# A fused attention and expert kernel: last batch's tiles reordered, an input split spread out, first step given more projection work

## The chip, the cores and the metric

One core of one Trainium2 chip runs the whole program. The metric is device time in microseconds for one execution, as the median of several runs.

## The reference

Three layers follow each other on four sequences of 576 tokens. The first two (windowed attention with 8 heads, then a gated layer with a spatial mix) are not touched by the change. The third is the one at issue:

```python
logits = x @ w_gate                      # 4 experts, the best 2 are kept, softmax over them
for e in range(E):
    q, k, v = x @ wq[e], x @ wk[e], x @ wv[e]
    a = softmax(causal(scale * (q @ k.T)))
    out += gate[e] * (a @ v @ wo[e])     # gate is 0 for experts that were not kept
```

Each expert is thus one causal attention head of width 64 over 576 tokens, weighted by a gate for each token.

## The kernel before, in words

The first 336 us compute the first two layers and the fold of their last weight into the projections. The change touches only what follows, the third layer, called stage B here.

Stage B has 20 tiles: four batches of five tiles of query rows, tiles 0 to 3 with 128 rows each and tile 4 with the last 64 rows (two experts stand side by side in it). Tile j sees j + 1 blocks of 128 keys, so tile 0 is the smallest and tiles 3 and 4 the largest. Tile 4 of two neighbouring batches share one output tile, so an even batch's tile 4 has no output work of its own.

The loop over s (L957) runs 22 steps. Step s does, in this order: `attend_b` of tile s - 2 (the product with v, into pxB, L906), the first half of `scores_b` of tile s (psB, L845, for tile 4 L847), `take_b` of tile s - 2 (pxB split into a rounded high part by ACT, L132, and a remainder by DVE, L129), and then five rounds, in each of which it takes some dense work (`dense.pull`), one group of up to four transposes of tile s - 1 (`turn_b`: TensorE into ptB, L888, copied to pTB by ACT or DVE, L889), and in two of the rounds the softmax of a half of tile s (`softmax_b`). The softmax of a half is a DVE operation with a running minimum (L150, for tile 4 L859), an exponential with row sums on ACT (L151, L861), then for both halves together L866 to L868 on DVE (sum, reciprocal, times the gate of the token), and the scaling of each row block by POOL (`scale_rows`, L158). The transposes read what POOL has scaled.

The dense work is a queue of generators: the projections of the next batch (`proj`: q and k, 12 matmuls of 288 columns for each half row, L780, evicted by ACT L784 and DVE L129; v and gate logits, L804, evicted by ACT L808) and the output tiles (`out_tile`: six matmuls of 512 columns, L927, evicted by ACT L941, written by SP L943). A unit is four of these matmuls (two in an output tile). `dense.pull(RATE / 5)` adds to a credit and hands out units until it is used up, so RATE is the dense work of a step in ns by the kernel's own count (488 for a unit of q or k). RATE is 3700 to step 14 and 4400 from there.

At the end of a projection `gates` computes the token gates of its batch from the logits (DVE L746 to L759, with one small POOL operation, L154, and a reciprocal, L155). Step 0 differs from the other steps that begin a batch: batch 0 was projected just ahead of the loop, so its gates are computed while step 0 runs, and L868 of tile (0, 0) waits for them.

`load_g` reads the input of a batch two ahead from memory (L699, L700) and splits it into a rounded part and a remainder, in four pieces: ACT L704 and DVE L129 for each, named x<-gf. They are handed out by `next(gparts)` in the rounds. The split of batch 3 overwrites what the projection of batch 1 reads, so it can't run before that has ended.

TensorE's instructions stand in the order in which the program calls them. For ACT, DVE, POOL and SP a scheduler sets the order when the kernel is built. The PSUM pools hold one score tile (psB), two tiles for transposes (ptB), one for pxB and three for dense work.

```python
for i in range(5):
    dense.pull((RATE if s < 15 else 4400.0) / 5)
    next(turn, None)
    ...
    if s < 15:
        next(gparts, None)
```

Of the kernel before, what the change touches and what calls it, by code (L numbers as in the profile page):

```python
# [21 lines left out]
B, H, S, D = 4, 8, 576, 64  # L22
# [80 lines left out]
def block_kernel(ctx, tc, qP, kP, v, w_in, wspT, bsp, w_outT, wcat, wo, rel, relt, low, tri, out):  # L103
    nc = tc.nc
# [20 lines left out]
    dense = Dense()  # L125
# [401 lines left out]
    tiles = [(b, j) for b in range(B) for j in range(5)]  # L527
# [75 lines left out]
    RATE = 8200.0  # L603
    outw = iter(())
    for s in range(2, len(tiles) + 2):
# [6 lines left out]
        if s > 2:  # L612
            b, j = tiles[s - 2]
# [306 lines left out]
    def out_tile(b, t):  # L920
        t0, tn = TOK[t][0], P
        o2 = OT.pop((b, t))
        po = psD.tile([P, 512], F32, tag="D", name=f"pout{b}_{t}")
        n = 0
        for i, j in PASSES:
            for pr in range(2):
                nc.tensor.matmul(po[:tn], o2[i][:, pr, :tn], wos[j][:, pr, :], start=(n == 0), stop=(n == 5))  # L927
                n += 1
            if n < 6:
                yield 2 * 216  # L930
        ot = wk.tile([P, DM], F32, tag="ot", name=f"ot{b}_{t}", bufs=3)
        if (b, t) == (B - 1, 4):

            for h, copy in enumerate((nc.scalar.copy, nc.vector.tensor_copy)):
                c = slice(256 * h, 256 * h + 256)
                copy(ot[:, c], po[:, c])  # L936
                for i in range(2):
                    (nc.sync, nc.scalar)[i].dma_start(out[b - 1 + i, t0:S, c], ot[64 * i : 64 * i + 64, c])
            yield 2 * 216
            return  # L940
        nc.scalar.copy(ot[:tn], po[:tn])  # L941
        if t < 4:
            nc.sync.dma_start(out[b, t0 : t0 + tn, :], ot)  # L943
        else:
            for i in range(2):
                nc.sync.dma_start(out[b - 1 + i, t0:S, :], ot[64 * i : 64 * i + 64])
        yield 2 * 216

    tiles = [(b, j) for b in range(B) for j in range(5)]
    dense.add(proj(0, G), 18000.0)  # L950
    G, gparts = load_g(1, gfp)
    for _ in gparts:
# [2 lines left out]
    RATE = 3700.0  # L955
    px = None
    for s in range(len(tiles) + 2):  # L957
        if s < len(tiles):
            b, j = tiles[s]
            if j == 0:  # L960
                dense.through(f"p{b}")
                for _ in gparts:
                    pass
                if b + 1 < B:
                    dense.add_front(proj(b + 1, G), 18000.0, f"p{b + 1}")
                if b + 2 < B:
                    G, gparts = load_g(b + 2, gfp)
        if s >= 2:
            px = attend_b(*tiles[s - 2])
        if s < len(tiles):  # L970
            scores_b(*tiles[s], 0)
        if s >= 2:
            b1, j1 = tiles[s - 2]
            take_b(b1, j1, px)
            if j1 < 4 or b1 % 2:
                dense.add(out_tile(b1, j1), 1300.0)
        turn = turn_b(*tiles[s - 1]) if 1 <= s <= len(tiles) else iter(())
        for i in range(5):
            dense.pull((RATE if s < 15 else 4400.0) / 5)
            next(turn, None)  # L980
            if s < len(tiles) and i == 0:
                softmax_b(*tiles[s], 0)
            if s < len(tiles) and i == 2:
                scores_b(*tiles[s], 1)
                softmax_b(*tiles[s], 1)
            if s < 15:
                next(gparts, None)
    dense.drain()

# [71 lines left out]
```

## Time and profile before

| | us |
|---|---|
| median of 3 runs (lowest to highest) | 515.16 (515.05 to 515.49) |
| the profiled execution, whole | 514.89 |
| its span, first to last recorded instruction | 513.2 |
| TensorE's matmuls busy in the span | 488.0 |

The page gives the busy time of each engine over the span. In a timeline each row is a run of equal instructions of one engine: start in us, length in us until the last of them has ended, engine, line, operation, tiles, shape and count, and in square brackets how long the engine had been idle and what released it. Matmuls are pipelined: the next row of TensorE starts some 0.1 to 0.25 us before the row ahead has ended, so the cost of a row is the distance from its start to the next row's start.

### The profile page before, as it was taken

How to read it: one execution, taken by the hardware profiler on the slowest of the kernel's cores; microseconds unless marked ns; L12 is line 12 of the kernel's file. 1: busy time of each engine (PE TensorE's matmuls, PEld its weight loads, DVE VectorE, ACT ScalarE, POOL GpSimd, SP SyncE). 2: the span in 40 equal slices, each digit the busy share in tenths (PEclk: the TensorE clock that was granted, in tenths of full speed). 3: DMA queues.
4: the chain of work that ended last, by engine and by line, in shares of the span. 5: the costliest groups of instructions: out<-in, count | busy, mean ns of one | idle time of the engine just before them, and what ended most of it. 6: DMA issues, size and time to landing. Idle time of an engine off the chain costs nothing. (4 is left out here: it accounts for less than half of the span.)

```text
span 513.2 us, 10541 instructions
## 1 busy us (share of the span) xinstructions
PE 488.0 (95%) x3910; PEld 425.5 (83%) x3910; DVE 308.4 (60%) x1069; ACT 261.8 (51%) x778; POOL 98.4 (19%) x205
## 2 busy tenths in 40 slices
PE   8879889999999999999999999989989999999995
PEld 6547668898988989899888999978978898897784
DVE  4978877555878768785455525264574564562441
ACT  4764567533656337463344314264564554546652
POOL 0012210222102211012211010122322333232121
PEclk9997989999999999999999999999999999999999
DMA  8931223325231451301206640230000000003321
GB/s 283 372 128 42 63 87 102 114 70 181 91 94 43 180 189 42 94 2 52 104 1 193 198 158 5 90 93 1 1 1 3 2 1 1 1 2 116 112 103 42
DMA packets 25079, 44.34 MB, mean 86 GB/s; under 512 B 5826, under 2 KB 8258, under 8 KB 24644
## 3 DMA queue, kind: packets, MB, share of 16 engines
q1 hardware_dynamic: 24868, 43.54, 25.4%
q8 instruction: 31, 0.51, 0.4%
q10 hardware_dynamic: 160, 0.13, 0.1%
q14 instruction: 20, 0.16, 0.1%
HBM read 32.13 MB, written 11.53 MB: 85 GB/s over the span
## 5 line engine op out<-in xcount | busy, mean ns | idle before, releaser
L151 ACT ACTIVATE p<-p,st 128x128 f32<-128x128 f32 x144 | 56.3, 392 | 38.0 <-DVE st L150 38.0
L436 PE MATMUL pv<-win,x 128*128 128x512 f32 x240 | 63.9, 409 | 0.7 <-ACT x L132 0.7
L780 PE MATMUL pq<-x,W 128*128 128x288 f32 x384 | 59.4, 303 | 0.9 <-DVE k L129 0.8
L516 PE MATMUL pg<-wsp,vn 128*128 128x288 f32 x384 | 58.9, 298 | 0.1
L780 PEld LDWEIGHTS pq<-x,W 128*128 128x128 f32 x384 | 52.1, 188 | 4.8 <-issue 2.3
L499 PE MATMUL pu<-x,win 128*128 128x288 f32 x384 | 55.1, 298 | 0.0
L398 POOL TENSOR_SCALAR_AFFINE_SELECT pU<-pT 128x512 f32<-128x512 f32 (+1 forms) x32 | 22.6, 706 | 168.1 <-ACT pT L391 164.1
L158 POOL TENSOR_SCALAR pB<-pB,stB 128x128 f32<-128x128 f32 (+4 forms) x72 | 39.0, 560 | 80.1 <-DVE stB L868 65.5
L516 PEld LDWEIGHTS pg<-wsp,vn 128*128 128x128 f32 x384 | 52.9, 188 | 1.3 <-issue 1.0
L499 PEld LDWEIGHTS pu<-x,win 128*128 128x128 f32 x384 | 52.0, 188 | 1.8 <-issue 0.5
L436 PEld LDWEIGHTS pv<-win,x 128*128 128x128 f32 x240 | 43.9, 192 | 9.8 <-issue 1.0
L151 ACT ACTIVATE pB<-pB,stB 128x128 f32<-128x128 f32 (+3 forms) x64 | 35.6, 558 | 13.6 <-DVE stB L150 13.6
L150 DVE CUSTOM_DVE_ANT_0 pB<-psB,trit 128x128 f32<-128x128 f32 (+3 forms) x64 | 28.3, 485 | 11.1 <-PE psB L845 10.5
L888 PE MATMUL ptB<-ident,pB 128*128 128x128 f32 (+1 forms) x200 | 31.1, 274 | 3.9 <-POOL pB L158 3.6
L804 PE MATMUL pvB<-W,x 128*128 128x260 f32 (+1 forms) x240 | 34.7, 289 | 0.0
L804 PEld LDWEIGHTS pvB<-W,x 128*128 128x128 f32 (+1 forms) x240 | 30.1, 178 | 1.1 <-issue 1.1
L927 PE MATMUL pout<-wo,o 128*128 128x512 f32 x108 | 30.1, 410 | 1.0 <-ACT o L132 1.0
L353 PE MATMUL ps<-k,q 64*128 64x256 f32 (+1 forms) x256 | 29.8, 374 | 0.8 <-DMA k<-in_kP 0.8
L390 PE MATMUL pt<-ident,p 128*128 128x128 f32 x144 | 22.9, 277 | 7.8 <-DVE x L129 6.1
L888 PEld LDWEIGHTS ptB<-ident,pB 128*128 128x128 f32 (+1 forms) x200 | 23.7, 139 | 7.6 <-POOL pB L158 4.7
L150 DVE CUSTOM_DVE_ANT_0 p<-ps,relm 128x128 f32<-128x128 f32 x128 | 29.5, 286 | 0.7 <-DMA relm<-in_rel 0.2
L415 PE MATMUL px<-pT,v 128*64 128x128 f32 (+1 forms) x320 | 29.6, 276 | 0.0
(147 smaller groups left out, 882.0 us busy)
## 6 DMA issues: line engine op xcount, KB each, us to landing
q<-in_qP SPq DMA_DIRECT2D x20, 256.0 KB, 3.0
g_dram<-g SPq DMA_DIRECT2D x16, 288.0 KB, 2.1
raw<-in_w_in SPq DMA_DIRECT2D x8, 512.0 KB, 6.8
v<-in_v SPq DMA_DIRECT2D x16, 256.0 KB, 3.2
gf<-g_dram SPq DMA_DIRECT2D x4, 1024.0 KB, 5.3
out<-ot SPq DMA_DIRECT2D x16, 256.0 KB, 2.0
k<-in_kP SPq DMA_DIRECT2D x3, 1152.0 KB, 5.3
rawo<-in_w_outT SPq DMA_DIRECT2D x4, 512.0 KB, 4.3
```

Of the source, the lines that this page charges most:

```text
L150: nc.vector.tensor_tensor_reduce(s_view, ps_view, tab, -0.125, FLT_MAX, ALU.add, ALU.min, nm)
L151: nc.scalar.activation(s_view, s_view, AF.Exp, bias=nm, scale=-1.0, accum_out=sm)
L158: nc.gpsimd.tensor_scalar(p, p, r, 0.0, op0=ALU.mult, op1=ALU.add)
L353: nc.tensor.matmul(ps[:, o, 256 * h : 256 * h + kn], Q_[b, j][r, hp, :], K_[b][r, hp, k0 : k0 + kn], start=True, stop=True)
L415: nc.tensor.matmul(px[64 * o : 64 * o + 64, hp, :qn], V_[b, t][:kb, h * 64 : h * 64 + 64], rhs, start=(t == max(0, j - 1)), stop=(t == j))
L436: nc.tensor.matmul(pv, x[i][:, k, t0 : t0 + P], win[j][:, k, 512:1024], start=(n == 0), stop=(n == 11))
L499: nc.tensor.matmul(pu[:, :HALF], win[i][:, k, m * P : (m + 1) * P], x[j][:, k, c], start=(n == 0), stop=(n == 11))
L516: nc.tensor.matmul(pg[:, :HALF], vn[i][k][:, m * P : (m + 1) * P], wsp[j][:, k, c], start=(n == 0), stop=False)
L780: nc.tensor.matmul(pq[:, :HALF], W[i][:, k, c0 : c0 + P], G[j][:, k, c], start=(n == 0), stop=(n == 11))
L804: nc.tensor.matmul(pv[:tn, :260], G[i][:, k, COL[t] : COL[t] + tn], W[j][:, k, 512:772], start=(n == 0), stop=(n == 11))
L888: nc.tensor.transpose(pt[:kb, n, :], p[pr][:, o, c0 : c0 + kb], ident)
L927: nc.tensor.matmul(po[:tn], o2[i][:, pr, :tn], wos[j][:, pr, :], start=(n == 0), stop=(n == 5))
```

## The change

Four edits, all in stage B. The tiles of the last batch (3) are taken in the order 3, 4, 2, 1, 0. The split of the input is handed out in rounds 1 and 3 of the steps that don't begin a batch, eight pieces over four steps, where it was one in every round from the beginning. In step 0 the dense credit is 5500 where it was 3700. And the last output tile, now tile 0 of batch 3 with 128 rows of one batch, is written as two halves of 256 columns, the first by SP and the second by ACT's queue, one transfer each, where the old last tile sent two transfers from each queue.

```diff
--- before.py
+++ after.py
@@ -929,13 +929,12 @@
             if n < 6:
                 yield 2 * 216
         ot = wk.tile([P, DM], F32, tag="ot", name=f"ot{b}_{t}", bufs=3)
-        if (b, t) == (B - 1, 4):
+        if (b, t) == tiles[-1]:
 
             for h, copy in enumerate((nc.scalar.copy, nc.vector.tensor_copy)):
                 c = slice(256 * h, 256 * h + 256)
                 copy(ot[:, c], po[:, c])
-                for i in range(2):
-                    (nc.sync, nc.scalar)[i].dma_start(out[b - 1 + i, t0:S, c], ot[64 * i : 64 * i + 64, c])
+                (nc.sync, nc.scalar)[h].dma_start(out[b, t0 : t0 + tn, c], ot[:, c])
             yield 2 * 216
             return
         nc.scalar.copy(ot[:tn], po[:tn])
@@ -946,7 +945,8 @@
                 nc.sync.dma_start(out[b - 1 + i, t0:S, :], ot[64 * i : 64 * i + 64])
         yield 2 * 216
 
-    tiles = [(b, j) for b in range(B) for j in range(5)]
+
+    tiles = [(b, j) for b in range(B) for j in ((3, 4, 2, 1, 0) if b == B - 1 else range(5))]
     dense.add(proj(0, G), 18000.0)
     G, gparts = load_g(1, gfp)
     for _ in gparts:
@@ -957,7 +957,7 @@
     for s in range(len(tiles) + 2):
         if s < len(tiles):
             b, j = tiles[s]
-            if j == 0:
+            if s % 5 == 0:
                 dense.through(f"p{b}")
                 for _ in gparts:
                     pass
@@ -976,14 +976,16 @@
                 dense.add(out_tile(b1, j1), 1300.0)
         turn = turn_b(*tiles[s - 1]) if 1 <= s <= len(tiles) else iter(())
         for i in range(5):
-            dense.pull((RATE if s < 15 else 4400.0) / 5)
+
+            dense.pull((5500.0 if s < 1 else RATE if s < 15 else 4400.0) / 5)
             next(turn, None)
             if s < len(tiles) and i == 0:
                 softmax_b(*tiles[s], 0)
             if s < len(tiles) and i == 2:
                 scores_b(*tiles[s], 1)
                 softmax_b(*tiles[s], 1)
-            if s < 15:
+
+            if s < 15 and s % 5 and i in (1, 3):
                 next(gparts, None)
     dense.drain()
```

**TensorE at the first two steps.** The piece from the last projection units of step 0 to the transposes of tile (0, 0). pq is a projection tile of batch 1, psB0_1 the scores of tile (0, 1), ptB0_0 the transposes of tile (0, 0). Before:

```order
L780 MATMUL pq1_0_0_0_3923<-x20_3582,W0_3250 128x288 x4
L780 MATMUL pq1_0_0_0_3923<-x21_3583,W0_3250 128x288 x4
L845 MATMUL psB0_1_0_3937<-k0_0_3612,q0_0_3614 128x256 x2
L845 MATMUL psB0_1_0_3937<-k0_1_3613,q0_0_3614 128x256 x2
L845 MATMUL psB0_1_0_3937<-k0_0_3612,q0_1_3615 128x256 x2
L845 MATMUL psB0_1_0_3937<-k0_0_3612,q0_0_3614 128x256 x2
L845 MATMUL psB0_1_0_3937<-k0_1_3613,q0_0_3614 128x256 x2
L845 MATMUL psB0_1_0_3937<-k0_0_3612,q0_1_3615 128x256 x2
L780 MATMUL pq1_0_0_0_3923<-x20_3582,W1_3251 128x288 x4
L780 MATMUL pq1_0_0_1_3960<-x20_3582,W0_3250 128x288 x4
L888 MATMUL ptB0_0_0_3965<-ident_72,pB0_0_0_3851 128x128 x2
L888 MATMUL ptB0_0_0_3965<-ident_72,pB0_0_1_3852 128x128 x2
```

After the change:

```order
L780 MATMUL pq1_0_0_1_3939<-x20_3582,W0_3250 128x288 x4
L780 MATMUL pq1_0_0_1_3939<-x21_3583,W0_3250 128x288 x4
L780 MATMUL pq1_0_0_1_3939<-x20_3582,W1_3251 128x288 x4
L845 MATMUL psB0_1_0_3956<-k0_0_3612,q0_0_3614 128x256 x2
L845 MATMUL psB0_1_0_3956<-k0_1_3613,q0_0_3614 128x256 x2
L845 MATMUL psB0_1_0_3956<-k0_0_3612,q0_1_3615 128x256 x2
L845 MATMUL psB0_1_0_3956<-k0_0_3612,q0_0_3614 128x256 x2
L845 MATMUL psB0_1_0_3956<-k0_1_3613,q0_0_3614 128x256 x2
L845 MATMUL psB0_1_0_3956<-k0_0_3612,q0_1_3615 128x256 x2
L780 MATMUL pq1_1_1_0_3970<-x20_3582,W0_3250 128x288 x4
L888 MATMUL ptB0_0_0_3975<-ident_72,pB0_0_0_3851 128x128 x2
L888 MATMUL ptB0_0_0_3975<-ident_72,pB0_0_1_3852 128x128 x2
```

Four more units stand ahead of the scores of (0, 1) and one fewer between them and the transposes: three more, all told, ahead of the transposes.

**DVE at the end of batch 0.** The rows from the split of batch 3 on. x21<-gf3 are its four remainders, pTB0_3 copies of transposes of tile (0, 3), stB0_4 the statistics of tile (0, 4), c1, c2 and mx the gates of batch 1. Before:

```order
L889 COPY pTB0_3_4_4277<-ptB0_3_4_4276 128x512
L859 ISA pB0_4_1_4238,stB0_4_4239<-psB0_4_1_4300,tritail_3255 128x288
L859 ISA stB0_4_4239 128x1
L859 ISA pB0_4_1_4238,stB0_4_4239<-psB0_4_1_4300,tritail_3255 128x288
L859 ISA stB0_4_4239 128x1
L889 COPY pTB0_3_12_4321<-ptB0_3_12_4320 128x512
L860 TENSOR_TENSOR stB0_4_4239<-stB0_4_4239 128x1
L129 TENSOR_TENSOR x21_3583<-gf3_4361,x20_3582 128x576 x4
L746 TENSOR_TENSOR c1_1_4332<-vt1_4142 128x80
L747 TENSOR_TENSOR c2_1_4333<-vt1_4142 128x80
L751 TENSOR_REDUCE mx1_4336<-vt1_4142 128x5
L866 TENSOR_SCALAR stB0_4_4239<-stB0_4_4239 128x2
```

After the change:

```order
L129 TENSOR_TENSOR x21_3583<-gf3_4373,x20_3582 128x576
L889 COPY pTB0_3_4_4294<-ptB0_3_4_4293 128x512
L129 TENSOR_TENSOR x21_3583<-gf3_4373,x20_3582 128x576 x2
L859 ISA pB0_4_1_4255,stB0_4_4256<-psB0_4_1_4339,tritail_3255 128x288
L859 ISA stB0_4_4256 128x1
L859 ISA pB0_4_1_4255,stB0_4_4256<-psB0_4_1_4339,tritail_3255 128x288
L859 ISA stB0_4_4256 128x1
L129 TENSOR_TENSOR x21_3583<-gf3_4373,x20_3582 128x576
L746 TENSOR_TENSOR c1_1_4301<-vt1_4114 128x80
L747 TENSOR_TENSOR c2_1_4302<-vt1_4114 128x80
L751 TENSOR_REDUCE mx1_4305<-vt1_4114 128x5
L889 COPY pTB0_3_12_4361<-ptB0_3_12_4360 128x512
```

The four remainders stood together behind the last copy of tile (0, 3) and the second softmax half of tile (0, 4); now three of them stand ahead of that half and the fourth right behind it, and the copy pTB0_3_12 has come behind all four. Further down L868 of tile (0, 4) has moved from behind the four L150 of tile (1, 0) to ahead of them, and five operations of the gates of batch 1 (L749, L750, L752, L756, L757) now stand ahead of it. The split of batch 2, the other one that the loop hands out, stands at the same places as before on ACT and DVE.

**ACT at the end of the program.** ot is the eviction of an output tile, pTB a copy of transposes, o the high part of an attended tile. Before, the last rows but one:

```order
L132 CAST o3_3_0_6003<-pxB3_3_5986 128x256
L941 COPY ot3_3_6014<-pout3_3_6007 128x512
L889 COPY pTB3_4_0_6018<-ptB3_4_0_6017 128x512
L889 COPY pTB3_4_8_6032<-ptB3_4_8_6031 64x256
L132 CAST o2_4_0_5643<-pxB3_4_6036 128x2x64
L936 COPY ot3_4_6066<-pout3_4_6059 128x256
L938 DMA out_0<-ot3_4_6066 64x256 x2
```

After the change:

```order
L132 CAST o3_2_0_5978<-pxB3_2_5949 128x256
L151 ACTIVATE pB3_0_0_5962,stB3_0_5964<-pB3_0_0_5962,stB3_0_5964 128x128 x2
L151 ACTIVATE pB3_0_1_5963,stB3_0_5964<-pB3_0_1_5963,stB3_0_5964 128x128 x2
L940 COPY ot3_2_5989<-pout3_2_5982 128x512
L889 COPY pTB3_1_0_5993<-ptB3_1_0_5992 128x512
L132 CAST o3_1_0_6030<-pxB3_1_6021 128x256
L940 COPY ot3_1_6041<-pout3_1_6034 128x512
L889 COPY pTB3_0_0_6045<-ptB3_0_0_6044 128x512
L132 CAST o3_0_0_6056<-pxB3_0_6051 128x256
L936 COPY ot3_0_6067<-pout3_0_6060 128x256
L937 DMA out_0<-ot3_0_6067 128x256
```

The exponentials of the last tile (L151) and the evictions of the output tiles now alternate with the copies that TensorE waits for: the eviction of pout3_2 stands ahead of the copy pTB3_1_0, and that of pout3_1 ahead of pTB3_0_0. On TensorE the end is now: pxB3_2, psB3_0, pout3_2, ptB3_1 (two groups), pxB3_1, pout3_1, ptB3_0, pxB3_0, pout3_0, with no other dense work between them; it was pxB3_3, pout3_3, ptB3_4 (two groups and a short one), pxB3_4, pout3_4.

## Rows read from the trace of the kernel before

**Rows 1.** The page, engines: busy us (share of the span) and instructions

```profile
PE 488.0 (95%) x3910; PEld 425.5 (83%) x3910; DVE 308.4 (60%) x1069; ACT 261.8 (51%) x778; POOL 98.4 (19%) x205
```

**Rows 2.** Waits from 335 us on: waiting, releaser, us in total, times, longest

```profile
PE ptB L888 <- POOL pB L158: 3.6, 2, 1.9
```

**Rows 3.** Timeline of TensorE, steps 0 and 1

```profile
335.94 0.88 PE L845 MATMUL psB<-k,q 64*128 64x128 f32 x12
336.75 4.49 PE L780 MATMUL pq<-x,W 128*128 128x288 f32 x32
341.18 0.98 PE L845 MATMUL psB<-k,q 64*128 64x256 f32 x12
342.08 1.32 PE L780 MATMUL pq<-x,W 128*128 128x288 f32 x8
345.33 1.37 PE L888 MATMUL ptB<-ident,pB 128*128 128x128 f32 x4 [1.92 <-POOL pB L158]
346.46 3.43 PE L780 MATMUL pq<-x,W 128*128 128x288 f32 x24
```

**Rows 4.** Timeline of all engines, same stretch: the gates of batch 0

```profile
342.23 0.24 POOL L154 TENSOR_SCALAR sm<-sm 128x5 f32<-128x5 f32 x1 [13.31 <-DVE sm L757]
...
342.92 0.40 ACT L784 CAST q<-pq 128x288 fp32r<-128x288 f32 x1 [2.09 <-PE pq L780]
...
343.40 0.54 POOL L792 TENSOR_SCALAR qt<-q 64x64 fp32r<-64x64 f32 x2 [0.93 <-ACT q L784]
...
343.64 0.17 DVE L759 TENSOR_TENSOR gt<-ex,sm 128x20 f32<-128x20 f32 x1
...
344.90 3.23 POOL L158 TENSOR_SCALAR pB<-pB,stB 128x128 f32<-128x128 f32 x8
```

**Rows 5.** Timeline of TensorE, step 5: transposes of tile (0, 4)

```profile
380.25 0.66 PE L888 MATMUL ptB<-ident,pB 128*128 128x128 f32 x4 [1.70 <-POOL pB L158]
...
381.28 0.60 PE L888 MATMUL ptB<-ident,pB 128*128 128x128 f32 x4
381.63 1.30 PE L780 MATMUL pq<-x,W 128*128 128x288 f32 x8
```

**Rows 6.** Timelines of ACT, DVE and POOL before step 5's transposes

```profile
372.90 2.40 ACT L704 CAST x<-gf 128x576 fp32r<-128x576 f32 x4 [0.27 <-PE pvB L804]
...
374.37 2.76 DVE L129 TENSOR_TENSOR x<-gf,x 128x576 fp32r<-128x576 f32 x4
...
379.45 1.47 POOL L158 TENSOR_SCALAR pB<-pB,stB 128x576 f32<-128x576 f32 x2 [6.33 <-DVE rk L750]
```

**Rows 7.** Timeline of TensorE, the end

```profile
499.25 1.97 PE L906 MATMUL pxB<-pTB,vt 128*64 128x128 f32 x32
501.80 1.68 PE L927 MATMUL pout<-wo,o 128*128 128x512 f32 x6 [0.58 <-ACT o L132]
...
505.02 1.82 PE L906 MATMUL pxB<-pTB,vt 128*64 128x64 f32 x40
507.21 1.66 PE L927 MATMUL pout<-wo,o 128*128 128x512 f32 x6 [0.37 <-ACT o L132]
```

**Rows 8.** Timeline of ACT and its DMA queue, the end

```profile
503.56 0.59 ACT L941 COPY ot<-pout 128x512 f32<-128x512 f32 x1 [1.81 <-issue]
...
504.04 0.59 ACT L889 COPY pTB<-ptB 128x512 f32<-128x512 f32 x1
...
509.36 1.40 ACTq L938 DMA_DIRECT2D out<-ot  x2
```

**Rows 9.** Timelines of ACT and DVE in step 10: four exponentials of a tile 0

```profile
420.63 0.40 ACT L151 ACTIVATE pB<-pB,stB 128x128 f32<-128x128 f32 x1 [1.78 <-DVE stB L150]
...
422.31 0.17 DVE L866 TENSOR_SCALAR stB<-stB 128x4 f32<-128x4 f32 x1 [1.03 <-ACT pB L151]
```

**Rows 10.** Windows, early in the program: length, busy by engine, granted TensorE clock, DMA

```profile
35.00:40.00 5.00, 2.45 (x24) 2.24 (x23) 4.93 (x19) 3.17 (x11) 1.82 (x3) 0.71 0.00 0
```

**Rows 11.** Timeline of TensorE, the same stretch

```profile
37.90 0.70 PE L415 MATMUL px<-pU,v 128*64 128x128 f32 x4 [2.55 <-ACT pT L391]
```

## The prediction

> **What bounds the kernel now.** Read the page first: TensorE's matmuls are busy for 95% of the span and no other engine comes near that [rows 1]. So an edit pays only if it takes away time in which TensorE stands still, or delays it. The waits from 335 us on, where the changed code begins, come next: of what TensorE's matmuls waited for there, one pair is large, transposes that waited for POOL's scaling, 3.6 us in two waits [rows 2]. The timelines tell where the two are. The first is in step 1, idle for 1.92 us, and the four transposes then come one by one as POOL delivers its rows [rows 3]. The second is at the head of step 5, idle for 1.70 us [rows 5]. Between them and the end TensorE's rows follow each other with no idle time until the last ten microseconds, where it stands for 0.58 and 0.37 us while ACT rounds an attended tile [rows 7]. These are the three places where the change can act. Everything else it moves is TensorE work that is done anyway, sooner or later.
>
> **Part 1, more projection work in step 0: -2.5 us.** A unit of four matmuls costs 0.554 us: 32 matmuls take from 336.75 to 341.18 [rows 3]. From 336.75 to the unit behind the transposes at 346.46 pass 9.71 us. The work in it is 8 units (4.43), the scores of (0, 1) (341.18 to 342.08, 0.90), two units (1.11) and four transposes (0.35, the distance from 381.28 to 381.63 [rows 5]), together 6.79. So 2.92 us are lost there, more than the 1.92 that stand in the bracket, because the transposes trickle in. After the change 12 units stand ahead of the scores and one behind: TensorE reaches the transposes at 336.75 + 6.65 + 0.90 + 0.55 = 344.85.
>
> Is POOL ready by then? The chain is: the gate (L759, ended at 343.81), L868, POOL's scaling from 344.90, a transpose 0.43 behind the first row [rows 3, 4]. The gate was late because the L150 of (0, 1) stood ahead of it on DVE; in the new order they stand behind. What holds it now is POOL, where two small copies of q (L792) have come ahead of the gate's own operation (L154). Those need the ninth unit, ended at about 341.9, then ACT's rounding (0.40), the copies (0.54) and L154 (0.24) [rows 4]: about 343.2. Two DVE operations of some 0.2 each bring the gate to 343.65, two tiny copies and L868 bring POOL's scaling to 344.05. Its rows come 0.35 apart (four in the 1.37 of the transposes, less the first [rows 3]), so the fourth transpose can go at 344.05 + 0.43 + 1.05 = 345.53 and the next unit at 345.63. Without a wait it would be 345.20. Lost: 0.4 in place of 2.9, a gain of 2.5. Bounds: 2.9 if POOL is early enough to hide everything, and 1.7 if the scaling starts at 344.90 as it did, for then three more units (3 x 0.554) are done by 346.46. I take 2.5, since the L150 have left the chain by order.
>
> **Part 2, the split of batch 3 moved: -1.1 us.** Before, DVE was held by four remainders from 374.37 to 377.13, and what TensorE waited for, POOL's scaling behind L868 of (0, 4), began at 379.45, the transposes at 380.25. TensorE had been ready since 378.55 [rows 5, 6]. The projection of batch 1 now ends earlier: its last unit that reads the rounded input stands three units, two groups of transposes and a score half further forward in TensorE's order, 3 x 0.55 + 0.70 + 0.90 = 3.25 us by the prices above. So ACT's first rounding can go at about 369.65, where it went at 372.90. The four remainders follow one rounding (0.6) later, and with the 2.76 they take and some 1.5 of a copy and a softmax half between them they end at about 374.6, which is 2.5 earlier. Of that 1.4 is given back: five gate operations have come ahead of L868, some 0.2 each like L759 [rows 4], and the second exponential of (0, 4) starts later than DVE could use it, since L860 stands behind the moved copy. POOL begins 1.1 sooner and the transposes start at 379.15. Bounds: 1.7, the whole wait, and 0, if what has come ahead of L868 takes all. The copy pTB0_3_12, now behind the four remainders and three gate operations, ends at about 375.9. The last quarter of pxB0_3 needs it. Reckoned back from 378.55 by two units, scores of 0.81 and 1.90 for the 32 matmuls [rows 3, 7], pxB0_3 starts at 374.6 and that quarter at 376.0. So the copy costs nothing, though by 0.1; it is what is late next.
>
> The split of batch 2 keeps its place on both engines, so that edit does nothing for it. From step 6 to 18 the distances between a softmax and its transposes change by at most one unit, and POOL ended well ahead there; I cost that at nothing; if the cover is gone at one of these places it costs the one unit, 0.55.
>
> **Part 3, the order 3, 4, 2, 1, 0: +1.1 us.** Before, from pxB3_3 at 499.25 to the end of the last output tile at 508.87 pass 9.62 us [rows 7]. The work is 1.90, 1.52 (an output tile to its follower), ten transposes 0.87, 1.75 and 1.66: 7.70. Lost: 1.9. The new order ends with small tiles, and since part 1 has brought dense work forward, none is left to lie between their hand-offs. Count from the start of pxB3_2. It ends at 1.5, the scores of (3, 0) (0.81, from 335.94 to 336.75 [rows 3]) at 2.3, and pout3_2 runs to 3.8. DVE starts on the scores at 2.4, ACT's exponentials at 2.7, and they hold ACT for 1.7, to 4.4 (420.63 to 422.31 [rows 9]). Only then does ACT evict pout3_2, and 0.48 later copy the transposes (503.56 to 504.04, then 0.59 long [rows 8]): ready at 5.5. TensorE had its transposes done at 4.5 and **loses 1.0**. pxB3_1, half the matmuls of the 1.97 row and some drain, ends at 6.6; rounding takes 0.45, **lost**; pout3_1 runs from 7.05 to 8.6, the four transposes to 8.95. ACT evicts pout3_1 from 8.8 and copies until 9.9: **0.95 lost**. pxB3_0 ends at 10.6, rounding 0.45 and some drain, **0.5 lost**, and pout3_0 ends at 12.7. Lost: some 3.0, against 1.9. Bounds: +0.5, if copy and eviction come in better order or overlap than I have them, and +2.4, if two of the four stand as long as the longest wait of the trace, 1.92 [rows 3]. I take 1.1. In the steps ahead of this the large tile 3 comes first in the batch; its scaled rows come 0.6 us ahead of their transposes by the same count, so nothing is added.
>
> **Part 4, the last write: -0.2 us.** ACT's queue spent 1.40 us on two issues [rows 8]. It now has one, which waits for DVE's half of the eviction (0.4 behind ACT's) and takes half of the 1.40: it ends about 0.25 sooner. It carries twice the bytes. Bounds -0.5 and +0.3.
>
> Sum: -2.5 - 1.1 + 1.1 - 0.2 = **-2.7 us** on the profiled execution, 514.89 (span 513.2). That execution lies 0.27 below the median, so against 515.16 I expect **512.5**. With all bounds at their ends the sum lies between -4.6 and +1.0.
>
> **The rivals.**
>
> *A cheap end.* The evictions hide better than I count, and the new end loses no more than the old. For it: ACT has little else to do there. Against: its order is fixed, with each eviction ahead of a copy. Then -3.8, 511.4.
>
> *The second wait stays.* The edit to the split takes DVE time from one place of a chain and puts it at another: L868 is still late, and pTB0_3_12 is late next. For it: DVE has no gap left from the first remainder to L868. With an end at +1.9 and part 1 at -2.3 that gives -0.6: 514.5, no change that shows.
>
> *Slower: TensorE's clock falls in the end.* Four hand-offs in twelve microseconds leave TensorE standing for a quarter of the time. Early in this program it stood for 2.55 us, the granted clock of that stretch was 0.71, a mean between its two levels, 2.4 and 1.2 GHz, and four matmuls took 0.70 [rows 10, 11]. In stage B 32 of the same shape take 1.97, four with the drain some 0.3 [rows 7]. Against it: behind the 1.92 us in step 1 the units cost as much as ahead of it (24 matmuls in 3.43 [rows 3]), and I count no gap over 1.0. It decides if a gap in the end grows beyond 1.92, towards 2.55. From pout3_1 on 1.52 + 0.35 + 0.6 + 1.66 = 4.1 us of work would cost double, +4.1 less some waits that it hides, about 3.8: 516.3. The Trainium skill has a rule for this, in "TensorE: Matmul & The Clock Gate", section "HAM oscillation — how this bites in real kernels": a kernel whose matmul bursts are parted by waits falls back to the slow clock again and again. By that rule this change is a bad one; the trace of before bears it out early in the program and not in stage B.
>
> **How the numbers follow.** The sum as worked out has a chance of 0.63, its own range being 511.5 to 513.9; the cheap end 0.12; the second wait that stays 0.17; the slow clock 0.06; 0.02 are left. A measurement of this kernel tells some 0.2% from no change, which is 1.03 us: 514.13 and 516.19 are the borders. Nearly all of the first, all of the second and a third of the third case are faster: 0.76. The rest of the third and the edge of the first are the same: 0.17. Slower: 0.07, the clock and what is left. The range 511.0 to 514.6 leaves out the clock case, the upper edge of the third and the lower edge of the second.
>
> **What would show it.** In the profile after: at the transposes of (0, 0) an idle time under 0.6 us, with the gate ahead of the L150 of (0, 1); at the transposes of (0, 4) between 0.3 and 1.2 us; at the end four idle times of TensorE before pxB3_1, pout3_1, pxB3_0 and pout3_0, some 3 us together, with a granted clock of 1.00. The prediction is wrong if the first wait is still over 1.5 us, if TensorE stands before the last quarter of pxB0_3, or if the end loses under 1.9 or over 4.5 us.

## The result, and the profile after

The changed kernel takes **510.41 us** (median of 4 runs, 509.65 to 510.64) against 515.25 for the kernel before beside it: a ratio of 0.9903, 95% interval 0.9886 to 0.9921. It is faster, as forecast, but by 4.8 us where 2.7 were forecast, and it lies below the range. The profiled execution took 510.52 us with a span of 508.8, against 514.89 and 513.2: 4.4 us less in the span. The page of the profile after, TensorE first [rows 1]:

```profile
PE 486.7 (96%) x3910; PEld 425.1 (84%) x3910; DVE 308.4 (61%) x1069; ACT 261.3 (51%) x778; POOL 98.2 (19%) x205
```

The work is the same; TensorE's idle time is what changed. The waits of its matmuls from 335 us on, all of them (waiting, releaser, us in total, times, longest):

```profile
PE pxB L906 <- ACT pTB L889: 1.4, 2, 0.8
PE pout L927 <- ACT o L132: 0.9, 2, 0.5
```

The pair that waited for POOL, 3.6 us [rows 2], is gone. What is left stands in the last ten microseconds.

**The first two steps.** TensorE's timeline after, from the projection units of step 0 to the first unit behind the transposes of (0, 0) [rows 3]:

```profile
336.93 6.59 PE L780 MATMUL pq<-x,W 128*128 128x288 f32 x48
343.46 0.98 PE L845 MATMUL psB<-k,q 64*128 64x256 f32 x12
344.36 0.80 PE L780 MATMUL pq<-x,W 128*128 128x288 f32 x4
345.00 1.06 PE L888 MATMUL ptB<-ident,pB 128*128 128x128 f32 x4
345.82 0.38 PE L780 MATMUL pq<-x,W 128*128 128x288 f32 x1
```

Twelve units stand ahead of the scores, the bracket with 1.92 us is gone, and the four transposes still come one by one: 0.82 us to the next row for 0.35 of work. That next unit starts 8.89 us after the first one, with three more units done ahead of it than before, where it was 9.71. The gain is 9.71 + 3 x 0.554 - 8.89 = 2.48 us. The chain behind it came as it was worked out: the gate of batch 0 (L759) ended at 343.78 and POOL's scaling began at 344.26, where 343.65 and 344.05 were forecast and stage B starts 0.18 later.

**Step 5.** TensorE's timeline after, two projection units and the first transposes of (0, 4) [rows 5]:

```profile
376.86 1.33 PE L780 MATMUL pq<-x,W 128*128 128x288 f32 x8
378.07 0.66 PE L888 MATMUL ptB<-ident,pB 128*128 128x128 f32 x4
```

No bracket: the whole 1.70 us is gone. From these two units to the transposes pass 1.21 us; before it was 3.02 (377.23 to 380.25 [rows 5]), so 1.81 are gained. The row of the two units in the kernel before:

```profile
377.23 1.32 PE L780 MATMUL pq<-x,W 128*128 128x288 f32 x8
```

DVE's timeline after, the last remainder of the split (L129) and the chain to L868, with two gate operations (L756, L757) and the remainder of an attended tile (L129, o) between; POOL's row behind it [rows 6]:

```profile
373.41 0.76 DVE L129 TENSOR_TENSOR x<-gf,x 128x576 fp32r<-128x576 f32 x1
...
376.21 0.17 DVE L866 TENSOR_SCALAR stB<-stB 128x2 f32<-128x2 f32 x1
376.32 0.18 DVE L756 TENSOR_TENSOR ex<-ex,rk 128x20 f32<-128x20 f32 x1
376.41 0.16 DVE L867 RECIPROCAL stB<-stB 128x2 f32<-128x2 f32 x1
376.53 0.17 DVE L757 TENSOR_REDUCE sm<-ex 128x5 f32<-128x20 f32 x1
376.62 0.41 DVE L129 TENSOR_TENSOR o<-pxB,o 128x256 fp32r<-128x256 f32 x1
376.95 0.15 DVE L868 TENSOR_TENSOR stB<-stB,gq 128x2 f32<-128x2 f32 x1
```

```profile
377.27 1.47 POOL L158 TENSOR_SCALAR pB<-pB,stB 128x576 f32<-128x576 f32 x2 [0.23 <-DVE sm L155]
```

POOL starts 2.18 us earlier than before. In the kernel before, the same chain ran from L866 to L868 in 1.70 us, with the four L150 of tile (1, 0) between them, of which the first is shown; now it takes 0.74:

```profile
377.43 0.16 DVE L866 TENSOR_SCALAR stB<-stB 128x2 f32<-128x2 f32 x1
...
378.14 0.27 DVE L150 CUSTOM_DVE_ANT_0 pB<-psB,trit 128x128 f32<-128x128 f32 x1
...
379.13 0.15 DVE L868 TENSOR_TENSOR stB<-stB,gq 128x2 f32<-128x2 f32 x1
```

A gate operation between two steps of the chain costs next to nothing. L867 starts 0.20 us after L866 with L756 between them (376.21 to 376.41), and 0.21 after it where nothing stands between, as in this place of the changed kernel:

```profile
357.09 0.17 DVE L866 TENSOR_SCALAR stB<-stB 128x4 f32<-128x4 f32 x1 [0.90 <-ACT pB L151]
357.30 0.18 DVE L867 RECIPROCAL stB<-stB 128x4 f32<-128x4 f32 x1
```

**The middle.** Before, weight loads of batch 3's projection waited twice for DVE to empty a projection tile. The weight-load timeline of the kernel before:

```profile
423.76 1.09 PEld L780 LDWEIGHTS pq<-x,W 128*128 128x128 f32 x8 [0.26 <-DVE k L129]
...
432.21 0.57 PEld L780 LDWEIGHTS pq<-x,W 128*128 128x128 f32 x4 [0.34 <-DVE q L129]
```

After the change neither stands there. (One load waits 0.25 for DVE's k at 431.28; the load in the same place before, at 434.24, was as long idle.) TensorE's matmul rows have no bracket for such a wait, since the row ahead has not ended yet; there it shows as length alone. The 12 matmuls that the first of the two waits falls into take 2.06 us to the next row (422.96 to 425.02), and after the change 12 such matmuls take 1.76 (420.68 to 422.44). From pxB1_3 to pxB2_3 the trace of before takes 41.18 us with two output matmuls in it that take 0.55 together, the trace after 40.06 with none: 0.57 less for equal work.

**The end.** TensorE's timeline after, from the attended product of (3, 2) on [rows 7], and the last row of ACT's queue [rows 8]:

```profile
492.38 1.53 PE L906 MATMUL pxB<-pTB,vt 128*64 128x128 f32 x24
...
496.15 1.03 PE L888 MATMUL ptB<-ident,pB 128*128 128x128 f32 x8
497.86 1.09 PE L906 MATMUL pxB<-pTB,vt 128*64 128x128 f32 x16 [0.68 <-ACT pTB L889]
499.43 1.66 PE L927 MATMUL pout<-wo,o 128*128 128x512 f32 x6 [0.47 <-ACT o L132]
500.93 0.60 PE L888 MATMUL ptB<-ident,pB 128*128 128x128 f32 x4
502.29 0.66 PE L906 MATMUL pxB<-pTB,vt 128*64 128x128 f32 x8 [0.77 <-ACT pTB L889]
503.42 1.66 PE L927 MATMUL pout<-wo,o 128*128 128x512 f32 x6 [0.47 <-ACT o L132]
```

```profile
506.02 0.37 ACTq L937 DMA_DIRECT2D out<-ot  x1
```

Four hand-offs, each with its idle time, and 12.70 us in all (492.38 to 505.08). From there to the end of the span pass 3.72 us, where it was 4.33 (508.87 to 513.2).

### The profile page after: what moved, and what is told of

The parts are those of the page before. It is cut to its first block, busy times and chain, and to the rows that moved or that the text cites. A ratio compares the mean times of both kernels' runs of the same rounds, so it can differ in the third digit from the quotient of the medians.

```text
span 508.8 us, 10533 instructions
## 1 busy us (share of the span) xinstructions
PE 486.7 (96%) x3910; PEld 425.1 (84%) x3910; DVE 308.4 (61%) x1069; ACT 261.3 (51%) x778; POOL 98.2 (19%) x205
## 4 chain that ended last, share of the span: by engine, by line
PE 77%; DVE 10%; ACT 6%; DMA 4%; issue 1%; SPq 1%; ACTq 0%
PE pg L516 10%; PE pv L436 10%; PE pq L780 10%; PE pu L499 6%; PE pvB L804 6%; PE pxB L906 5%; PE pout L927 5%; PE px L415 4%; PE ptB L888 4%; PE psB L845 4%; PE pw L679 3%; PE ps L353 3%; PE pt L390 2%; ACT p L151 2%; PE pg L521 2%; DMA raw<-in_w_in 2%
## 5 line engine op out<-in xcount | busy, mean ns | idle before, releaser
L151 ACT ACTIVATE p<-p,st 128x128 f32<-128x128 f32 x144 | 56.3, 392 | 37.6 <-DVE st L150 37.6
L780 PE MATMUL pq<-x,W 128*128 128x288 f32 x384 | 58.3, 302 | 0.8 <-DVE k L129 0.8
L151 ACT ACTIVATE pB<-pB,stB 128x128 f32<-128x128 f32 (+3 forms) x64 | 35.7, 559 | 21.4 <-DVE stB L150 21.4
L150 DVE CUSTOM_DVE_ANT_0 pB<-psB,trit 128x128 f32<-128x128 f32 (+3 forms) x64 | 28.2, 486 | 9.9 <-PE psB L845 9.2
L150 DVE CUSTOM_DVE_ANT_0 p<-ps,relm 128x128 f32<-128x128 f32 x128 | 29.5, 285 | 0.7 <-DMA relm<-in_rel 0.2
L906 PE MATMUL pxB<-pTB,vt 128*64 128x128 f32 (+2 forms) x480 | 28.3, 262 | 1.4 <-ACT pTB L889 1.4
L353 PE MATMUL ps<-k,q 64*128 64x256 f32 (+1 forms) x256 | 28.6, 363 | 0.6 <-DMA k<-in_kP 0.6
```

The costliest lines, as they stand in the source:

```text
L150: nc.vector.tensor_tensor_reduce(s_view, ps_view, tab, -0.125, FLT_MAX, ALU.add, ALU.min, nm)
L151: nc.scalar.activation(s_view, s_view, AF.Exp, bias=nm, scale=-1.0, accum_out=sm)
L353: nc.tensor.matmul(ps[:, o, 256 * h : 256 * h + kn], Q_[b, j][r, hp, :], K_[b][r, hp, k0 : k0 + kn], start=True, stop=True)
L780: nc.tensor.matmul(pq[:, :HALF], W[i][:, k, c0 : c0 + P], G[j][:, k, c], start=(n == 0), stop=(n == 11))
L906: nc.tensor.matmul(px[64 * o : 64 * o + 64, pr, :qn], vt[:kb, c, (2 * pr + o) * 64 : (2 * pr + o) * 64 + 64], rhs, start=(c == 0), stop=(c ...
```

## The experiments

In all of them the same four stretches of the profiled execution are compared: from the first scores of stage B to pxB1_3, to pxB2_3, to the end of the last output matmul, and the rest of the span. Each is a distance between two starts (or to an end) in TensorE's timeline. Where a kernel does dense work earlier, it is in an earlier stretch; the column "stage B" is free of that.

| kernel | to pxB1_3 | to pxB2_3 | to last matmul | stage B | rest | median us | ratio (95%) |
|---|---|---|---|---|---|---|---|
| before | 80.52 | 41.18 | 51.23 | 172.93 | 4.33 | 515.25 | |
| changed | 78.62 | 40.06 | 50.28 | 168.96 | 3.72 | 510.41 | 0.9903 (0.9886 to 0.9921) |
| a2_after | 78.62 | 40.06 | 50.32 | 169.00 | 3.73 | 510.17 | 0.9892 (0.9872 to 0.9911) |
| e1_rate | 78.65 | 40.06 | 50.84 | 169.55 | 4.29 | 510.83 | 0.9904 (0.9892 to 0.9917) |
| e3_order | 82.06 | 41.15 | 51.38 | 174.59 | 3.68 | 515.13 | 0.9985 (0.9975 to 0.9994) |
| e9_step1 | 81.07 | 40.09 | 50.28 | 171.44 | 3.74 | 513.66 | 0.9955 (0.9943 to 0.9967) |
| e5_write4 | 78.63 | 40.06 | 50.31 | 169.00 | 4.21 | 510.89 | 0.9902 (0.9884 to 0.9920) |
| e7_hold | 78.50 | 41.18 | 50.79 | 170.47 | 3.73 | 511.91 | 0.9922 (0.9910 to 0.9934) |
| e6_whole | 81.32 | 41.61 | 50.05 | 172.98 | 4.33 | 515.73 | 0.9998 (0.9984 to 1.0012) |
| e10_tail_b | 78.65 | 40.06 | 47.71 | 166.42 | 3.75 | 507.10 | 0.9842 (0.9823 to 0.9862) |
| e8_tail | 78.66 | 40.08 | 48.37 | 167.11 | 3.71 | 508.91 | 0.9878 (0.9861 to 0.9895) |
| e12_more | 78.67 | 40.06 | 48.33 | 167.06 | 3.77 | 508.18 | 0.9861 (0.9846 to 0.9876) |
| e11_old_order | 78.65 | 40.05 | 49.52 | 168.22 | 4.26 | 510.34 | 0.9901 (0.9886 to 0.9916) |

Each ratio is to runs of the kernel before on the same chip. The changed kernel's stage B came out at 168.96 and 169.00 in two executions. Its start in these executions lies between 335.12 and 336.69, in code that no kernel changes; that spread is in the times, and the stretches are free of it.

### e1_rate: the kernel before with 5500 in step 0 alone

```diff
-            dense.pull((RATE if s < 15 else 4400.0) / 5)
+            dense.pull((5500.0 if s < 1 else RATE if s < 15 else 4400.0) / 5)
```

> The 5500 in step 0 alone, everything else as before. Theory T: this one edit brings the gain at both waits and in the middle. Worked out from the two traces: -2.5 at the transposes of (0, 0), -1.8 at those of (0, 4), -0.6 in the projection of batch 3, where a half-done output tile no longer holds a PSUM buffer; against that some +1.6 at the end, which keeps the old tile order but has lost the output units that lay between its hand-offs. Sum -3.3: 512.0, range 511.2 to 512.8. Rival P, as predicted: the second wait is the split edit's and the middle is nothing, so this edit gives -2.5 and the end takes +0.5 or so: 513.3.

Neither of the two waits for POOL is there. TensorE's timeline of e1_rate at the transposes of (0, 4), and the longest idle time of its end (0.59 and 0.36 stand before the last two output tiles):

```profile
378.11 0.66 PE L888 MATMUL ptB<-ident,pB 128*128 128x128 f32 x4
...
494.31 0.63 PE L888 MATMUL ptB<-ident,pB 128*128 128x128 f32 x4 [1.03 <-ACT pTB L889]
```

So the number 5500 alone removes both waits, and the middle is as in the changed kernel, 40.06. The split has no part in it: with the split edit alone added to the kernel before, every engine's instructions stand in the order that they had; and so it is when it is added to e1_rate. Stage B is 3.38 us shorter than before's, as theory T's sum of -3.3 has it. The time, 510.83, came out below both expectations; the profiled execution was the longest of the four, 511.72.

### e3_order: the new order and the last write, without the 5500

```diff
-    tiles = [(b, j) for b in range(B) for j in range(5)]
+    tiles = [(b, j) for b in range(B) for j in ((3, 4, 2, 1, 0) if b == B - 1 else range(5))]
...
-                for i in range(2):
-                    (nc.sync, nc.scalar)[i].dma_start(out[b - 1 + i, t0:S, c], ot[64 * i : 64 * i + 64, c])
+                (nc.sync, nc.scalar)[h].dma_start(out[b, t0 : t0 + tn, c], ot[:, c])
```

> The order 3, 4, 2, 1, 0 with the new last write, and the split edit, which leaves the program as it is; credit 3700 in step 0. Theory T: both waits, 1.9 and 1.7, are there as before. The end has more output units left than after the whole change, two of them between the first hand-off: it loses 2 to 2.5 where the old one lost 1.9, and the last write gives 0.5. Sum 0: 515.2, range 514.5 to 516. Rival: the order pays by itself, the small last tile shortens the end by 1 or more: 514 or less.

The split edit, which the expectation counts in, is not in this kernel; it moves no instruction (e1_rate). Both waits are back, 1.92 and 1.70 us. The end is 0.15 longer than before, the rest 0.65 shorter: together 0.5 less, where the times show 0.3 to 1.3 less. Its first stretch is 1.54 longer than before for the same instructions in the same order. TensorE's timeline of e3_order, the 24 matmuls behind the first wait, where 3.43 stood before [rows 3], and the windows of that stretch (length, busy by engine, granted clock, DMA):

```profile
345.32 1.38 PE L888 MATMUL ptB<-ident,pB 128*128 128x128 f32 x4 [1.92 <-POOL pB L158]
346.46 4.96 PE L780 MATMUL pq<-x,W 128*128 128x288 f32 x24
```

```profile
347.00:348.00 1.00, 1.00 (x7) 1.00 (x7) 0.00 (x0) 0.33 (x1) 1.00 (x3) 0.64 0.00 0
348.00:349.00 1.00, 1.00 (x6) 1.00 (x5) 0.46 (x1) 0.40 (x1) 0.14 (x1) 0.50 0.06 16
...
351.00:352.00 1.00, 1.00 (x14) 0.67 (x12) 0.46 (x1) 0.33 (x1) 0.00 (x0) 1.00 0.00 0
```

The granted clock fell to 0.50, which is 1.2 GHz, behind the wait and came back some three microseconds later. In the profiled executions of the kernel before, e9_step1 and e6_whole, which have the same wait of 1.92, it stayed at 1.00 in this place.

### e9_step1: the changed kernel with the 5500 in step 1

```diff
-            dense.pull((5500.0 if s < 1 else RATE if s < 15 else 4400.0) / 5)
+            dense.pull((5500.0 if s == 1 else RATE if s < 15 else 4400.0) / 5)
```

> The whole change with the 5500 in step 1 in place of step 0. From step 2 on TensorE has the same rows. Theory T: the wait at (0, 0) is back (1.9 idle, 2.5 lost) and nothing else: the wait at (0, 4) stays away, because only the end of the projection of batch 1 decides it: 512.9, range 512.5 to 513.3. Rival (the second wait went because the first did, or the split edit took it): the wait at (0, 4) is back too by 1 or more, or 512 and less because the first stays away.

TensorE's timeline of e9_step1 at the transposes of (0, 0) and of (0, 4):

```profile
345.21 1.38 PE L888 MATMUL ptB<-ident,pB 128*128 128x128 f32 x4 [1.92 <-POOL pB L158]
...
380.22 0.66 PE L888 MATMUL ptB<-ident,pB 128*128 128x128 f32 x4
```

The first wait is back and the second stays away. So the first is filled by work that stands ahead of it, and the second goes because batch 1's projection ends earlier, wherever the extra units were taken. Stage B is 2.48 longer than in the changed kernel: the price of part 1, measured by itself. The time, 513.66, lies 0.4 above the range of theory T; by the trace its mechanism holds.

### e7_hold: the changed kernel with 5000 in step 0

```diff
-            dense.pull((5500.0 if s < 1 else RATE if s < 15 else 4400.0) / 5)
+            dense.pull((5000.0 if s < 1 else RATE if s < 15 else 4400.0) / 5)
```

> The whole change with 5000 in place of 5500, one unit less in step 0. By the order an output tile of batch 0 is then left unfinished, with its PSUM buffer, through the projections of batches 2 and 3; with 5500 it is finished ahead of the one of batch 3. Theory B (the buffer): TensorE's weight loads wait again for DVE in the projection of batch 3, some 0.6 in two waits as in the kernel before, and the first wait costs up to 0.4 more: 511.2, and the stretch from pxB1_3 to pxB2_3 is 0.5 to 0.6 longer than after the change at equal work. Rival (the waits came from where the units lay, not from the buffer): only the first wait, 510.6.

Two of the waits of weight loads in e7_hold between pxB1_3 and pxB2_3, those on a projection tile that DVE has yet to empty:

```profile
PEld pq L780 <- DVE q L129: 0.3, 1, 0.3
PEld pq L780 <- DVE k L129: 0.3, 1, 0.3
```

They are those of before, and the stretch is 41.18 again, with two output matmuls in it as before. With one unit less, pout0_1 is begun by two matmuls (in the kernel before it was pout0_0) and left so until batch 3's projection is through. It holds one of the three dense PSUM tiles, and the projection has two. The time, 511.91, is 0.7 above the expected 511.2: the stretch up to pxB1_3 lost 0.9 for equal work, where up to 0.4 was expected. The missing unit cost its whole 0.54 at the transposes of (0, 0), and 0.27 at those of (0, 4).

### e6_whole: the kernel before, output tiles taken in one piece

```diff
-                yield 2 * 216
+                pass
...
-        yield 2 * 216
+        yield 6 * 216
```

The `yield` of the last tile is changed in the same way.

> The kernel before with one edit: an output tile's six matmuls are taken in one piece, so that no half-done output tile can hold one of the three dense PSUM tiles. Theory B (the 0.6 us that the changed kernel gained in steps 6 to 18 come from the third PSUM tile that a half-done output tile held): the weight-load waits of 0.26 us on DVE's k and 0.34 us on DVE's q in the projection of batch 3 go away, and the stretch from pxB1_3 to pxB2_3 is 0.6 us shorter for equal work. The edit also pulls dense work into step 4, which fills up to 1.1 of the 1.70 us in front of the transposes of (0, 4), but takes it from the end, where up to 1.5 us more is lost: 514.0 to 515.3. Rival M (the 0.6 is from softmax and transposes of the middle that stand at other units): the weight-load waits stay and the stretch is as long as before.

The two weight-load waits are gone. The stretch, 41.61, holds six output matmuls that take 1.48 (458.14 to 459.62): 40.13 without them, where before it is 41.18 - 0.55 = 40.63. So 0.5 went with the half-done tile. The time did not fall below before's, and is above what was expected: the wait at (0, 4) is still 1.20, and the end has 2.04 us of idle times where before had 1.18. The mechanism holds; as a change it is worth nothing.

### e5_write4: the changed kernel with four transfers for its last tile

```diff
-                (nc.sync, nc.scalar)[h].dma_start(out[b, t0 : t0 + tn, c], ot[:, c])
+                for i in range(2):
+                    r = slice(64 * i, 64 * i + 64)
+                    (nc.sync, nc.scalar)[i].dma_start(out[b, t0 + 64 * i : t0 + 64 * i + 64, c], ot[r, c])
```

For comparison the changed kernel ran once more, as a2_after. What was expected of it, and then of e5_write4:

> The changed kernel once more, beside the three that follow, so that they are compared on one chip. Both theories: ratio to the kernel before 0.990, 510.4 us (510.0 to 511.0), lost 2.4 us in the four idle times of the end (0.68, 0.47, 0.77, 0.47).

> The changed kernel, but its last output tile is written as two transfers of 64 rows from each queue, as the kernel before wrote its last tile. Theory W (the 0.6 us between the end of the last output matmul and the end of the span come from the number of issues): ACT's queue holds the last issue 1.0 to 1.4 us instead of 0.37, the distance from the last matmul's end to the end of the span is 4.3 instead of 3.7 us, and the kernel takes 0.6 us more than the changed one. Rival V (the distance comes from which tile it is and from its eviction): 3.7 stays, no difference over 0.2.

The issues of e5_write4 by queue (duration in ns, least, median and most):

```profile
L939 SPq DMA_DIRECT2D out<-ot x2: 472/510/547, 505.7 to 506.2; - x2
L939 ACTq DMA_DIRECT2D out<-ot x2: 554/672/790, 505.7 to 506.3; - x2
```

a2_after, the changed kernel again, came out as expected. The stage B of e5_write4 is 169.00, the rest 4.21 where a2_after has 3.73: 0.5 us, as theory W has it in kind, 0.1 less in size. The times, 510.89 against 510.17, point the same way, but their intervals overlap (0.9884 to 0.9920).

### e10_tail_b, e8_tail, e12_more, e11_old_order: work kept for the end

```diff
-            dense.pull((5500.0 if s < 1 else RATE if s < 15 else 4400.0) / 5)
+            dense.pull((5500.0 if s < 1 else RATE if s < 15 else 3700.0 if s < 19 else 2200.0) / 5)
```

That is e10_tail_b. In e8_tail 3700.0 is 3800.0, in e12_more 5500.0 is 6000.0, and e11_old_order is the kernel before with e10_tail_b's numbers.

> The changed kernel, but the dense work of a step is 3700 up to step 18 and 2200 in the steps 19 to 21 (it was 4400 from step 15), so that output matmuls are left to stand in all four hand-offs of the end. Theory T (the four idle times are there because no dense work is left, and are filled if it is): of the 2.4 us in idle times under 1 is left, and the time is 508.0 to 509.0, faster than both kernels. Rival R (the hand-offs are only pushed on: ACT must evict the output tiles in the same stretch, so that its copies come later still): the idle times stay at 2 us or more in sum and the time at 510.0 to 511.0.

TensorE's timeline of e10_tail_b, from the output tile ahead of pxB3_1 to the end:

```profile
493.34 1.64 PE L927 MATMUL pout<-wo,o 128*128 128x512 f32 x6
494.91 1.09 PE L906 MATMUL pxB<-pTB,vt 128*64 128x128 f32 x16
495.93 0.73 PE L927 MATMUL pout<-wo,o 128*128 128x512 f32 x2
496.50 0.60 PE L888 MATMUL ptB<-ident,pB 128*128 128x128 f32 x4
496.86 2.09 PE L927 MATMUL pout<-wo,o 128*128 128x512 f32 x8
498.88 0.66 PE L906 MATMUL pxB<-pTB,vt 128*64 128x128 f32 x8
499.47 2.18 PE L927 MATMUL pout<-wo,o 128*128 128x512 f32 x8
```

No idle time stands before any matmul from 335 us on, the end is 2.57 shorter than the changed kernel's, and 507.10 us, below the range of theory T, beats both kernels.

> The changed kernel with 3800 in the steps 15 to 18 and 2200 from step 19: as e10_tail_b, but nothing stands between the attended product of the last tile and its output tile. Theory T: the one idle time of 0.47 us, with some drain around it 0.6, is back in that place and no other: 0.4 to 0.7 us over e10_tail_b. Rival R (the hand-off is covered in any case): the same time as e10_tail_b.

One idle time of 0.47 is back, before the last output tile, and the stage is 0.69 longer: theory T.

> As e10_tail_b, but 6000 in step 0, one unit of dense work more. Theory T (the first transposes still trickle in, 0.81 us for work of 0.35, since POOL's rows come 0.35 apart): one unit of 0.55 more stands ahead of them, the trickle goes, and 0.4 us is gained in step 1, while from there on 0 to 0.3 is lost in places that the unit now leaves: 0.0 to -0.4 us against e10_tail_b. Rival P (the unit brings another copy of q ahead of the gate's operation on POOL, so that the scaling starts later by as much): the trickle stays, no gain, 0 to +0.5.

TensorE's timeline of e12_more, the transposes of (0, 0) and the last output tile:

```profile
344.68 0.60 PE L888 MATMUL ptB<-ident,pB 128*128 128x128 f32 x4
345.03 1.17 PE L780 MATMUL pq<-x,W 128*128 128x288 f32 x7
...
500.68 1.65 PE L927 MATMUL pout<-wo,o 128*128 128x512 f32 x6 [0.47 <-ACT o L132]
```

The trickle is gone, 0.35 in place of 0.82, but the unit is missing later: 0.47 of idle time is back at the end, 0.26 stands before transposes at 460.52, and stage B is 0.64 longer than e10_tail_b's. The expectation that the later loss would stay under 0.3 was wrong.

> The kernel before with 5500 in step 0, then 3700 up to step 18 and 2200 in the steps 19 to 21; the order of the tiles and the last write are those of before. Theory T (what the end loses is set by how much dense work is left for its hand-offs, not by the order of its tiles): no idle time over 0.3 us in the end, stage B as long as with the new order and the same rates (166.4 us from its first scores to the end of its last matmul, give or take 0.4), the last write 0.5 us longer: 0.5 us over the kernel e10_tail_b, 507.6 to 509.0. Rival O (the new order is needed, since the last tile 4 has a long attended product and a rounding behind it with little left to lie there): over 1.5 us of idle time in the end, 509.5 to 510.5.

Both theories were partly wrong. The waits of e11_old_order's matmuls from 335 us on:

```profile
PE ptB L888 <- POOL pB L158: 0.8, 2, 0.5
PE ptB L888 <- ACT pTB L889: 0.3, 1, 0.3
```

The hand-offs of its end are filled, but transposes of the large last tiles now come before POOL has scaled their rows. Stage B is 1.80 longer than with the new order and the same rates, and 1.33 shorter than in e1_rate, the old order with the old rates at the end. So in the traces the work kept for the end pays with either order, and more with the new one (2.54). The ratios of e11_old_order and e1_rate, 0.9901 and 0.9904, don't tell the two apart.

## Why the prediction was wrong, point by point

**The change of the span, by the trace.** Part 1 -2.48; part 2 -1.81, and a further -0.19 in small pieces up to pxB1_3; the middle -0.57; the end +1.11 (it is 0.95 shorter, but holds eight output matmuls fewer, some 0.26 each); the last write -0.61; a start of stage B that is 0.18 later: -4.37, of the 4.4 seen.

**Part 1 was right**, -2.5 against -2.48, and e9_step1 has 2.48 as well. The next unit was put at 345.63 and came at 345.82, with stage B 0.18 later.

**Part 2 is the step that failed most**, in its cause and in its size: -1.1 was forecast and -1.81 came. The forecast credits "the split of batch 3 moved". The split edit moves no instruction. What moved the split is part 1's number, which ends batch 1's projection earlier (e1_rate, e3_order, e9_step1). The reasoning itself had the right reason in it (the unit that reads the rounded input stands 3.25 us further forward), under the wrong edit. And "of that 1.4 is given back" was mis-sized. The last remainder ended 2.96 earlier (374.17 for 377.13), where 2.5 was worked out, and POOL began 2.18 earlier, so that 0.78 was given back. The late second exponential was there as forecast: L866, which needs it, came 2.04 behind the last remainder, where it had come 0.30 behind. But the gate operations were charged with their length, 0.2 each. Three of the five (L749, L750, L752) ran before ACT's second exponential had ended at 376.18, which L866 comes behind; of the other two L756 cost nothing and L757 took 0.09 (376.53 to 376.62). And the forecast did not count that the four L150 of tile (1, 0) no longer stand between L866 and L868: 0.74 us in place of 1.70. A wait of 0.6 was forecast to remain; none does. "The second wait stays" is refuted.

**The middle, costed at nothing, was the other error.** The forecast looked at waits of matmuls and at POOL's lead. The 0.57 stood in waits of weight loads, and their cause was a PSUM tile held by a half-done output tile from step 4 to step 15. e7_hold brings the waits back with one unit less, e6_whole removes them by another way.

**Part 3 was right in its number**: 12.7 us from pxB3_2 forecast and measured, four idle times in the four places named, +1.1. This was not luck: counted from pxB3_2, what follows the four hand-offs came at 5.48, 7.05, 9.91 and 11.04, where 5.5, 7.05, 9.9 and 11.1 were worked out. Two idle times are shorter than computed (0.68 and 0.77 us for 1.0 and 0.95), not because the copies were ready sooner, but because the rows of the transposes ahead of them ended some 0.2 to 0.3 later. But the heading gives the loss to the order. e1_rate, with the old order, loses more: its end is 0.56 longer. The +1.1 is what part 1 took from the end, softened by the order. With the old rate the order costs 0.15 (e3_order).

**Part 4 was mis-sized**: -0.6 for -0.2, beyond its own bound of -0.5. The forecast halved the time of ACT's two issues; the one that is left takes 0.37 of their 1.40 us. With the four issues back, e5_write4 loses 0.5 again.

**The slower rival** did not happen: the windows of the end have a granted clock of 1.00. Its mechanism exists all the same, at the wait that the change removes (e3_order), and there behind 1.92 us: the forecast expected a fall only beyond that.

What stays open: by the stretches the order and the write together are worth 1.1 us over e1_rate (0.56 in the end, 0.57 in the rest). The times of e1_rate and of the changed kernel can't tell them apart.

## What to carry to other kernels

Before a gain is credited to an edit, see whether that edit moves any instruction at all; here one number brought the gain that the forecast had put down to two edits. When work is pulled forward to fill an early wait, count what it leaves at the end, and keep there as many pieces as the end has hand-offs: e10_tail_b's stage B is 2.5 us shorter than the changed kernel's for that alone. And look at the waits of weight loads too, where a buffer that is held too long shows when the matmuls' waits are silent.

## What the runs showed of the hardware

**The clock can fall behind a wait of 1.92 us.** In one of four profiled executions with this wait, the granted clock then fell to 0.50 (1.2 GHz), and 24 matmuls took 1.52 us more (346.46 to 351.34, where the kernel before has 346.46 to 349.82). Behind the four idle times of up to 0.77 us at the end of the changed kernel it did not fall. The Trainium skill, "TensorE: Matmul & The Clock Gate", section "HAM oscillation — how this bites in real kernels", says that waits between bursts of matmuls bring the slow clock back; e3_order agrees, at one wait, and three executions show that it need not come.

**An issue of 64 rows takes longer than one of 128.** One issue of 128 rows took 0.33 us on SP's queue and 0.37 on ACT's. Four issues of 64 rows, on both queues at once, took 0.47 to 0.79 each, and ACT's last one ended 1.38 us after its first began. On SP's queue this is not due to the other queue: its two took 1.11 us together, and two issues of 64 rows that the changed kernel makes there with no issue on ACT's queue take as long:

```profile
478.58 1.15 SPq L945 DMA_DIRECT2D out<-ot  x2
```

Why ACT's took longer still, 0.55 and 0.79, is open: no run has them alone. The Trainium skill, "DMA: Bandwidth & Descriptors", section "🎯 Rules for kernel authors", advises one transfer of 128 partitions over two of half of them; e5_write4 agrees, with 0.5 us.
